# Key-value sums over four tiles of tokens, and other figures for DMA additions in the planner of a gated attention kernel

## The chip, the cores and the metric

One core of one Trainium2 chip. The metric is the device time of one execution in microseconds. Before the change it is 724.36 us, the median of three executions (723.66 to 725.03).

## What is computed

Two attention branches over the same x (2048 tokens of 512, 32 heads of 16), mixed by a gate for each token. Projections and final weights are left out here except where they show:

```python
g = sigmoid((x * gate_w).sum(-1, keepdims=True))
# branch A, softmax attention
q, k, v = split_heads(x @ A_wqkv)
a = merge(softmax(q @ k.T * 16 ** -0.5) @ v) @ A_wo
# branch B, linear attention; w_phi is 16 x 16 for each head
q, k, v = split_heads(x @ B_wqkv)
phi = lambda t: concat(softmax(t @ w_phi), softmax(-(t @ w_phi)))   # 32 features
kv, z = phi(k).T @ v, phi(k).sum(tokens)
b = merge((phi(q) @ kv) / (phi(q) @ z + 1e-6)) @ B_wo
out = g * a + (1 - g) * b
```

## The kernel before

**Branch A** is nearly all of the work: 2048 x 2048 scores for each of 32 heads. A *unit* is 128 keys by 512 queries of one head; four units (four heads that sit in four row groups of TensorE) make a step, and 512 steps make the kernel. `_qk` (L1185 in `_scores`) writes scores of two units at a time to a ring of four PSUM banks, and `_exp` (L1233) takes their exponential on ScalarE into `ET`, a ring of 16 units in SBUF. `_pv` (L1296 in `_values`) multiplies a step's `ET` by V and adds it to a PSUM bank that is held for 16 steps; this group of 16 steps is one head slot of 512 queries. The exponential of a unit must wait until the value product of the unit 16 places before it has read its slot.

ScalarE is not alone with the exponentials. `NUMS` gives for each of the 32 groups a number of *batches* of four units that VectorE makes instead. VectorE writes the exponential's bits by arithmetic: one multiply-add from PSUM to 16-bit whole numbers in a tile `va` (L1043), and constants added to the whole numbers for further approximations in tiles `vb` (L1072 on VectorE, L1085 on GpSimd). Some of these additions are done by DMA: GpSimd issues a transfer that adds the constant tile `steps` to `va` or `vb` (L1077, 512 KB). Each batch takes four value products of its own (`pvx`, also L1296), and those of an added tile wait for the transfer to land.

**Branch B** goes through key tiles of 128 tokens first: `_b_pair` projects two tiles and makes their features in one of two slots of `bq` (L1457, L1475 to L1498 and, on ScalarE, the exponential L1494); `_b_v` makes the values (`VB`, four slots); `_b_kv` (L1573) multiplies features by values for two halves of the heads, and VectorE adds each result to `kvacc` (L1581, L1584). Then `_b_kvbd` lays the sums out, and the query tiles follow in pairs (L1613, L1633, L1663, L1668).

Projections of q and k for branch A are L808 (L816 and L855 for the first block of tokens), of v L923. L1303 and L1205 are filler matmuls on zeros or into banks that are overwritten, which keep TensorE busy. At the end `_out` projects both branches (L808 again) and stores the rows.

**The order of the work** is made by `Plan` when the program is built: every operation carries a cost, a latency, a due time and dependencies, and `order()` picks, over and over, the operation that can start first by its own clock, the more urgent one among equals. The order that it finds is then each engine's fixed program; semaphores make the engines wait for each other. Three of its tables and figures matter here:

- `SEEDS`: 64 numbers; every eight steps the next one shifts the due times of all operations that are still open by up to a few steps, at random. It is a choice among many orders of nearly equal merit.
- `SLIP`: `_late` holds back any TensorE work that would end after the moment at which the ring's next scores must start, and `SLIP` shifts that moment.
- `FIRST`, `MOVES`, `LANDED`: the planner's figures for one addition by DMA. Its transfer starts `FIRST` after the issue or when the one before it has moved, takes `MOVES`, and has landed `LANDED` later. Value products on the added tile are put in the order behind that moment.

```python
self.chan = max(t + self.FIRST, self.chan) + o.moves
o.lat = self.chan + self.LANDED - o.end
```

Of the kernel before, what the change touches and what calls it, by code (L numbers as in the profile page):

```python
# [70 lines left out]
class Plan:  # L71
# [6 lines left out]
    SWITCH, PASS, STEP = 0.097, 0.2155, 0.004  # L78
    SPAN, SHARE, FILL = 3.0, 0.58, 0.2155
    PAD, PADS, OVER = 0.45, 2, 0.2  # L80
    SLIP, GAPS, FLOOR = -0.015, 0.65, 0.46

    def __init__(self):
        self.ops = []
# [58 lines left out]
        self.ops.append(o)  # L143
        return o

    SEEDS = (46439, 36297, 2531, 40950, 971, 19659, 43523, 55019, 18035, 35534, 32147, 43513, 5583, 38153, 15135, 20962, 59679, 30439, 26213, 19105, 29455, 34877, 55135, 21414, 3210, 43195, 29993, 1363, 20599, 10691, 26101, 32053, 19915, 10799, 30427, 37694, 56714, 13257, 35679, 20623, 23887, 52907, 36031, 9619, 51019, 11311, 52185, 0, 13385, 43491, 31707, 19759, 44590, 53230, 9789, 22249, 59009, 3577, 57594, 35439, 52351, 16746, 45215, 2875)
    EVERY = 8
    FIRST, LANDED, TURN, HOLD = 1.5, 1.5, 1.9, 30.0

    def shift(self):  # L150

        if len(self.SEEDS) <= self.drawn or self.now < self.EVERY * self.drawn:
            return
        s = self.SEEDS[self.drawn]
        self.drawn += 1
# [329 lines left out]
class _Kernel:  # L485
# [11 lines left out]
    P_Q, P_MUL, P_NEG = 1, 1, 1  # L497
    P_REC, P_SUM = 0, 4
    P_BACK, RATIO, BV = 0, 1, 8
    DEN, KV2, P_MAX = 1, 0, 0  # L500
    P_SUB = 0
    REND = 4
    RINGOUT = 1
# [8 lines left out]
    LAST, FIRST_OUT, NEXT_OUT, DEP_OUT = 0, 3, 0, 2  # L512
    ALONE, EARLY = 12, 10
    C_MIX, C_POOL, SPREAD = 15.5, (0.2, 0.0011), 0.9
    C_ADD, MOVES, ADD_AT, PVD, U3 = 0.9, 2.9, -1, 0, 2
    L_MIX, L_BACK, L_PHIT, L_ONTB = 6.5, 0.4, 0.9, 0.4
    TWOS, BEGIN, SPLIT, PSPLIT = 2, 44, 262, 1
    PHIT2, ONTB2, C_PHIT2, C_ONTB2 = 1, 1, 2.3, 1.9
# [460 lines left out]
                prio=100))  # L979
        self.b_gB.writers = done  # L980

    NUMS = (1, 4, 5, 4, 4, 5, 4, 5, 4, 5, 4, 6, 5, 4, 4, 5, 5, 5, 5, 4, 4, 5, 4, 5, 4, 5, 5, 5, 6, 6, 5, 4)

    def _plan_vector(self):

        NT, away = self.NT, []
        for g in range(self.NPACK // NT):
            n = self.NUMS[g]
            rest = self.REND if g == self.NPACK // NT - 1 else self.REST
# [885 lines left out]
```

## Time and profile before

| | |
|---|---|
| median of three executions | 724.36 us (723.66 to 725.03) |
| the profiled execution | 723.53 us |
| its span, first to last instruction | 721.7 us |
| exponentials of branch A (L1233) | 734, of which 4 of half width |
| batches made by VectorE | 146 of four units |
| DMA additions (L1077) | 157 |
| additions to `kvacc` (L1584) | 14, and two first copies (L1581) |

PE is TensorE's matmuls, PEld its weight loads, DVE VectorE, ACT ScalarE, POOL GpSimd, SP the engine that issues other DMAs. A row of a group gives line, engine, operation, tiles written and read, shapes and count; then busy us and the mean ns of one; then the engine's idle us just ahead of them, with what ended most of it. A row of a timeline gives start, length, engine, line, and in brackets the idle time before it and its releaser. Records of ACT and DVE overlap their neighbours, so the distance of starts is shorter than a record.

### The profile page before, as it was taken

The numbers are of one execution on the slowest core, as the hardware profiler recorded it, in microseconds if no ns is written. First come the engines' busy times: TensorE is split into PE (matmuls) and PEld (weight loads), VectorE is DVE, ScalarE is ACT, GpSimd is POOL, SyncE is SP. The second block draws the span as 40 slices with busy tenths as digits, with TensorE's granted clock in tenths as the row PEclk, the third lists the DMA queues.
The fourth block names the chain that finished last, engine by engine and source line by source line (L and its number), as shares of the span: only waits on it lengthen the run. The fifth ranks groups of instructions, "written<-read, shape, count | busy, mean of one in ns | idle before, by whom it ended". The sixth has DMA issues, their size and how long they took to land.

```text
span 721.7 us, 17384 instructions
## 1 busy us (share of the span) xinstructions
PE 694.0 (96%) x7312; PEld 211.7 (29%) x7375; DVE 691.5 (96%) x1143; ACT 706.4 (98%) x756; POOL 447.8 (62%) x567
## 2 busy tenths in 40 slices
PE   8999999999999999999999999999999999999998
PEld 3332232222333222222222233232323232223222
DVE  4999999999999999999999999999999999999997
ACT  5999999999999999999999999999999999999996
POOL 3332566665675747485768775768758678477552
PEclk9999999999999999999999999999999999999999
DMA  9623676684966778966768877678678577868873
GB/s 226 155 50 74 123 136 119 116 158 94 189 117 118 147 143 169 187 121 118 140 122 157 166 146 146 105 147 159 114 135 163 112 155 147 151 129 150 165 139 88
DMA packets 68557, 99.17 MB, mean 137 GB/s; under 512 B 42752, under 2 KB 47872, under 8 KB 68480
## 3 DMA queue, kind: packets, MB, share of 16 engines
q0 software_dynamic: 22608, 82.32, 60.4%
q1 hardware_dynamic: 44000, 14.96, 10.3%
q8 instruction: 57, 0.93, 0.5%
q10 hardware_dynamic: 1872, 0.79, 0.5%
q14 instruction: 20, 0.16, 0.1%
HBM read 4.21 MB, written 2.10 MB: 9 GB/s over the span
## 4 chain that ended last, share of the span: by engine, by line
ACT 65%; PE 20%; DVE 7%; DMA 3%; POOL 2%; issue 1%; SPq 1%; POOLq 0%
ACT ET L1233 63%; PE ps L1185 7%; PE ps L1296 7%; PE ps L808 5%; ACT bq L1494 2%; DVE va L1043 2%; DVE vb L1072 1%; DMA va<-steps 1%; DMA vb<-steps 1%; SPq L673 1%; DMA xT<-in_A_x_dram 1%; DVE va_vb L1043 1%; POOL va L1077 0%; DVE onB L1668 0%; PE ps L923 0%
## 5 line engine op out<-in xcount | busy, mean ns | idle before, releaser
L1233 ACT ACTIVATE ET<-ps 128x1024 bf16<-128x1024 f32 (+1 forms) x734 | 677.1, 1084 | 3.1 <-PE ps L1185 1.6
L1043 DVE TENSOR_SCALAR va<-ps 128x512 uint16<-128x512 f32 (+1 forms) x438 | 312.6, 745 | 13.1 <-PE ps L1185 12.1
L1185 PE MATMUL ps<-qT,kT 32*128 32x512 bf16 (+1 forms) x2052 | 292.3, 384 | 13.3 <-ACT ET L1233 7.7
L1077 POOL DMA_DIRECT2D va<-steps x106 | 107.1, 1061 | 103.6 <-DVE vb L1072 50.2
L1185 PEld LDWEIGHTS ps<-qT,kT 32*128 32x128 bf16 x2052 | 74.0, 91 | 277.5 <-ACT ET L1233 255.8
L1296 PE MATMUL ps<-ET,V 128*32 128x512 bf16 x1464 | 141.9, 388 | 0.7 <-DVE va L1043 0.7
L1072 DVE TENSOR_SCALAR vb<-va 128x2048 uint16<-128x2048 uint16 x147 | 100.3, 695 | 0.2 <-PE ps L1296 0.2
L1296 PE MATMUL ps<-va,V 128*32 128x512 bf16 x984 | 92.3, 384 | 0.3 <-DVE vb L1072 0.3
L1296 PE MATMUL ps<-vb,V 128*32 128x512 bf16 x896 | 84.1, 384 | 0.6 <-DMA vb<-steps 0.3
L1085 POOL TENSOR_TENSOR vb<-vb,steps 128x512 int32<-128x512 int32 x50 | 64.0, 1299 | 26.7 <-DVE vb L1072 19.2
L1296 PEld LDWEIGHTS ps<-ET,V 128*32 128x32 bf16 x1464 | 36.4, 94 | 66.9 <-issue 59.0
L808 PE MATMUL ps<-WB,xT 128*128 128x512 bf16 x164 | 49.6, 383 | 3.6 <-issue 2.4
L1498 POOL TENSOR_TENSOR btree<-btree 128x512 f16<-128x512 f16 (+1 forms) x32 | 30.3, 947 | 22.2 <-DVE vb L1072 12.7
L1303 PE MATMUL ps<-kT,zero 128*32 128x512 bf16 x492 | 43.1, 383 | 0.0
L1077 POOL DMA_DIRECT2D vb<-steps x28 | 33.7, 1203 | 8.2 <-PE ps L808 3.7
L808 PE MATMUL ps<-xT,WA 128*128 128x512 bf16 x102 | 32.4, 384 | 2.0 <-issue 1.3
L1043 DVE TENSOR_SCALAR va_vb<-ps 128x512 uint16<-128x512 f32 (+1 forms) x47 | 33.7, 734 | 0.1
L1296 PEld LDWEIGHTS ps<-va,V 128*32 128x32 bf16 x984 | 24.3, 95 | 27.9 <-issue 20.8
L1494 ACT ACTIVATE bq<-bq 128x2048 bf16<-128x2048 bf16 x16 | 31.4, 1960 | 0.0
L899 POOL TENSOR_SCALAR qT<-qT,mask 128x512 bf16<-128x512 bf16 x30 | 22.8, 761 | 12.1 <-DVE qT L895 6.2
L1296 PEld LDWEIGHTS ps<-vb,V 128*32 128x32 bf16 x896 | 22.0, 95 | 24.3 <-issue 14.3
L1043 DVE TENSOR_SCALAR va_wt<-ps 128x512 uint16<-128x512 f32 (+1 forms) x36 | 25.9, 738 | 0.1
(123 smaller groups left out, 721.2 us busy)
## 6 DMA issues: line engine op xcount, KB each, us to landing
va<-steps POOLq DMA_DIRECT2D x106, 512.0 KB, 6.3
vb<-steps POOLq DMA_DIRECT2D x28, 512.0 KB, 7.0
va_wt<-steps POOLq DMA_DIRECT2D x10, 512.0 KB, 5.9
va_vb<-steps POOLq DMA_DIRECT2D x10, 512.0 KB, 5.5
WB<-in_B_wqkv_dram SPq DMA_DIRECT2D x1, 1536.0 KB, 8.2
vb_on<-steps POOLq DMA_DIRECT2D x3, 512.0 KB, 6.7
out_dram<-outt SPq DMA_DIRECT2D x12, 128.0 KB, 6.3
WA<-in_A_wqkv_dram SPq DMA_DIRECT2D x2, 384.0 KB, 4.4
```

The costliest lines, as they stand in the source:

```text
L808: return e.matmul(out, lhs, rhs, start=start, stop=stop)
L899: x = self.plan.op("POOL", lambda e, side=side: e.tensor_scalar(self.qT[:, s0 + side, :], raw, self.mask[:, side:side + 1], 0.0, op0=ALU.m ...
L1043: bits = lambda e, to, src: e.tensor_scalar(to, src, SCALE * LOG2E * 128.0, float(ORIGIN), op0=ALU.mult, op1=ALU.add)
L1072: o = op("DVE", lambda e: e.tensor_scalar(whole(dst), whole(va), float(by), None, op0=ALU.add), 0.16 + n * QCH * 0.00026, reads=reads, wri ...
L1077: o = self.dma("POOL", f"add{number}_{k}", lambda e: e.dma_start(tile[:, 0:n], self.steps[:, 0:n], accum_op=ALU.add), cost=self.C_ADD, rea ...
L1085: o = op("POOL", lambda e, lo=lo, hi=hi: e.tensor_tensor(whole(v3)[:, lo:hi].bitcast(I32), whole(v1)[:, lo:hi].bitcast(I32), whole(self.st ...
L1185: return e.matmul(out[:, cols], self.kT[32 * i:32 * i + 32, cp, kt * TOK:(kt + 1) * TOK], self.qT[32 * i:32 * i + 32, s, cols], start=True ...
L1233: o = plan.op("ACT", lambda e: e.activation(self.ET[:, a % NS:a % NS + n, cols], self.ps[:, a % NR:a % NR + n, cols], ACT.Exp, scale=SCALE ...
L1296: ins = e.matmul(self._bank(ot)[32 * i:32 * i + 32, :], v[:, v0:v0 + 32], tile, start=(kt == 0), stop=(kt == self.NT - 1), tile_position=( ...
L1303: ins = e.matmul(self._bank(ot)[32 * i:32 * i + 32, :], self.zero[:], self.kT[:, 0, 0:QCH], start=False, stop=False, tile_position=(0, 32 ...
L1494: op("ACT", lambda e: e.activation(flat, flat, ACT.Exp), 1.789, reads=[b], writes=[b], name="b_exp", prio=due + 1)
L1498: + [("b_sum", two(128 * n), lambda e, n=n: e.tensor_tensor(half[:, :, 0:n], half[:, :, 0:n], half[:, :, n:2 * n], ALU.add), (n <= self.P_ ...
```

## The change

`KV2` makes `_b_kv` wait for four tiles of tokens and add their products in PSUM, so 4 results for each half go to `kvacc` where 8 did. The planner takes additions to start, move and land sooner, and `SLIP` is stricter. `NUMS` gives VectorE 145 batches for 146, with one batch more in the first group and one fewer in the last. `SEEDS` is a new list throughout.

```diff
-    SLIP, GAPS, FLOOR = -0.015, 0.65, 0.46
+    SLIP, GAPS, FLOOR = -0.04, 0.65, 0.46
...
-    FIRST, LANDED, TURN, HOLD = 1.5, 1.5, 1.9, 30.0
+    FIRST, LANDED, TURN, HOLD = 1.4, 1.2, 1.9, 30.0
...
-    DEN, KV2, P_MAX = 1, 0, 0
+    DEN, KV2, P_MAX = 1, 1, 0
...
-    C_ADD, MOVES, ADD_AT, PVD, U3 = 0.9, 2.9, -1, 0, 2
+    C_ADD, MOVES, ADD_AT, PVD, U3 = 0.9, 2.85, -1, 0, 2
...
-    NUMS = (1, 4, 5, 4, 4, 5, 4, 5, 4, 5, 4, 6, 5, 4, 4, 5, 5, 5, 5, 4, 4, 5, 4, 5, 4, 5, 5, 5, 6, 6, 5, 4)
+    NUMS = (2, 4, 4, 5, 5, 5, 4, 4, 5, 5, 5, 4, 5, 6, 4, 6, 4, 6, 4, 4, 4, 4, 4, 5, 4, 4, 5, 4, 5, 6, 6, 3)
```

With the new due times nearly every row of the order moves. Three places on TensorE follow. Row by row they have line, operation, tile written and read, shape, and a count where equal ones follow each other.

The first is the start, up to the first value product (L1296). L1185 are scores of the ring and of the first batches, L808 the projections of k, L923 those of v. Before, the last 12 rows up to it:

```order
L808 MATMUL ps<-xT,WA 128x512 x2
L1185 MATMUL ps<-qT,kT 128x512 x2
L923 MATMUL ps<-WA,xT 128x2x128 x4
L1185 MATMUL ps<-qT,kT 128x512 x4
L923 MATMUL ps<-WA,xT 128x2x128 x4
L808 MATMUL ps<-xT,WA 128x512
L1185 MATMUL ps<-qT,kT 128x512 x2
L923 MATMUL ps<-WA,xT 128x2x128 x4
L1185 MATMUL ps<-qT,kT 128x512 x3
L923 MATMUL ps<-WA,xT 128x2x128 x4
L1185 MATMUL ps<-qT,kT 128x512 x3
L1296 MATMUL ps<-ET,V 32x512 x8
```

Now, likewise the last 12 rows (one more L923 x4 stands two rows ahead of them, and a filler L1205 ahead of the first full-width scores):

```order
L923 MATMUL ps<-WA,xT 128x2x128 x4
L1185 MATMUL ps<-qT,kT 128x512 x3
L923 MATMUL ps<-WA,xT 128x2x128 x4
L1185 MATMUL ps<-qT,kT 128x512 x3
L923 MATMUL ps<-WA,xT 128x2x128 x4
L808 MATMUL ps<-xT,WA 128x512
L1185 MATMUL ps<-qT,kT 128x512 x3
L808 MATMUL ps<-xT,WA 128x512 x2
L1185 MATMUL ps<-qT,kT 128x512 x3
L808 MATMUL ps<-xT,WA 128x512
L923 MATMUL ps<-WA,xT 128x2x128 x8
L1296 MATMUL ps<-ET,V 32x512 x4
```

Ahead of the first value product stand 24 matmuls of L923 where 16 stood; the other eight were right behind it. The matmuls of L808 between the first full-width scores and it are eight in both; four of them now stand behind the first L923, where one did.

The second is the end, from the last scores on. `ET` is ScalarE's tile, `va`, `vb`, `WB` those of VectorE's batches; L808 are the output projections of both branches. Before:

```order
L1185 MATMUL ps<-qT,kT 128x512 x2
L808 MATMUL ps<-WoA,onTA 128x512 x3
L808 MATMUL ps<-WoB,WT 128x512 x2
L1296 MATMUL ps<-ET,V 32x512 x4
L1296 MATMUL ps<-va_100,V_67 32x512 x4
L1296 MATMUL ps<-va_97,V_67 32x512 x4
L1296 MATMUL ps<-vb_104,V_67 32x512 x4
L808 MATMUL ps<-WoB,WT 128x512 x2
L808 MATMUL ps<-WoA,onTA 128x512 x6
L808 MATMUL ps<-WoB,WT 128x512 x4
L808 MATMUL ps<-WoA,onTA 128x512 x7
```

Now:

```order
L1185 MATMUL ps<-qT,kT 128x512 x2
L1296 MATMUL ps<-ET,V 32x512 x4
L1296 MATMUL ps<-va_100,V_67 32x512 x4
L1296 MATMUL ps<-ET,V 32x512 x4
L1296 MATMUL ps<-WB,V_67 32x512 x4
L1296 MATMUL ps<-ET,V 32x512 x8
L1296 MATMUL ps<-va_vb,V_67 32x512 x4
L808 MATMUL ps<-WoA,onTA 128x512 x4
L808 MATMUL ps<-WoB,WT 128x512 x8
L808 MATMUL ps<-WoA,onTA 128x512 x7
```

Seven value products follow the last scores where four did, and 19 projections where 24 did; behind the last exponential's own product (the last four of `ET`) one product stands ahead of the projections, not three.

The third is the first key-value sum (L1573, features `bq` by values `VB`), both halves of the heads. Before:

```order
L1185 MATMUL ps<-qT,kT 128x512 x2
L1573 MATMUL ps<-VB,bq 128x68 x8
L1185 MATMUL ps<-qT,kT 128x512 x4
L1296 MATMUL ps<-ET,V 32x512 x4
L1296 MATMUL ps<-vb_101,V_67 32x512 x4
L1296 MATMUL ps<-ET,V 32x512 x4
L1185 MATMUL ps<-qT,kT 128x512 x2
L1573 MATMUL ps<-VB,bq 128x68 x8
L1185 MATMUL ps<-qT,kT 128x512 x2
```

Now:

```order
L1185 MATMUL ps<-qT,kT 128x512 x2
L1573 MATMUL ps<-VB,bq 128x68 x16
L1185 MATMUL ps<-qT,kT 128x512 x3
L1296 MATMUL ps<-ET,V 32x512 x4
L1296 MATMUL ps<-vb_103,V_67 32x512 x4
L1296 MATMUL ps<-va_97,V 32x512 x4
L1185 MATMUL ps<-qT,kT 128x512 x3
L1296 MATMUL ps<-ET,V 32x512 x4
L1296 MATMUL ps<-vb_102,V_67 32x512 x4
L1185 MATMUL ps<-qT,kT 128x512 x2
L1573 MATMUL ps<-VB,bq 128x68 x16
L1185 MATMUL ps<-qT,kT 128x512 x3
```

A half's sum is one piece of 16 matmuls over four tiles where it was two pieces of 8 over two; there are 8 pieces of 16 in all, where 12 of 8 and 2 of 16 (two halves next to each other) stood.

More of the change, by code (lines that the diff above doesn't have):

```diff
@@ L144, in op @@
         return o
-    SEEDS = (46439, 36297, 2531, 40950, 971, 19659, 43523, 55019, 18035, 35534, 32147, 43513, 5583, 38153, 15135, 20962, 59679, 30439, 26213, 19105, 29455, 34877, 55135, 21414, 3210, 43195, 29993, 1363, 20599, 10691, 26101, 32053, 19915, 10799, 30427, 37694, 56714, 13257, 35679, 20623, 23887, 52907, 36031, 9619, 51019, 11311, 52185, 0, 13385, 43491, 31707, 19759, 44590, 53230, 9789, 22249, 59009, 3577, 57594, 35439, 52351, 16746, 45215, 2875)
+    SEEDS = (45959, 51639, 22027, 0, 55887, 32675, 45763, 19658, 23974, 59913, 48419, 50277, 38610, 29071, 54255, 16561, 28074, 8627, 30494, 39995, 2986, 24098, 45178, 38933, 24915, 36789, 25403, 3823, 12338, 46755, 9994, 14699, 28830, 13382, 17277, 24473, 47187, 46797, 29842, 24695, 38758, 30863, 50967, 40255, 29411, 50751, 30934, 36618, 21679, 35286, 15639, 9075, 55554, 30865, 8986, 8939, 45463, 37302, 49375, 44231, 4706, 52075, 15731, 25615)
     EVERY = 8
-    FIRST, LANDED, TURN, HOLD = 1.5, 1.5, 1.9, 30.0
+    FIRST, LANDED, TURN, HOLD = 1.4, 1.2, 1.9, 30.0
     def shift(self):
```

## The prediction, made blind

> **What bounds the kernel now.** First the page: busy time by engine, the chain that ended last, and the two dearest groups.
>
> ```profile
> span 721.7 us, 17384 instructions
> PE 694.0 (96%) x7312; PEld 211.7 (29%) x7375; DVE 691.5 (96%) x1143; ACT 706.4 (98%) x756; POOL 447.8 (62%) x567
> ACT 65%; PE 20%; DVE 7%; DMA 3%; POOL 2%; issue 1%; SPq 1%; POOLq 0%
> L1233 ACT ACTIVATE ET<-ps 128x1024 bf16<-128x1024 f32 (+1 forms) x734 | 677.1, 1084 | 3.1 <-PE ps L1185 1.6
> ```
>
> Three engines are nearly full, so the shares do not choose between them. The idle time before the exponentials does: 3.1 us before 734 of them, and the chain runs through ACT for 65%. Next the windows, three of them (columns: length; then busy us and instructions of PE, PEld, DVE, ACT, POOL; clock, DMA share, GB/s).
>
> ```profile
> 60.00:100.00 40.00, 39.12 (x361) 11.47 (x364) 38.78 (x68) 39.95 (x44) 20.44 (x29) 1.00 0.63 119
> 340.00:380.00 40.00, 38.12 (x425) 11.01 (x425) 38.26 (x64) 40.00 (x44) 27.38 (x40) 1.00 0.69 131
> 660.00:700.00 40.00, 39.18 (x443) 11.41 (x444) 38.36 (x64) 40.00 (x45) 21.22 (x21) 1.00 0.85 161
> ```
>
> ACT is busy for the whole of each, while PE and DVE each leave 0.8 to 1.9 us. But records of ACT overlap, so "busy" hides small delays. For the true pace I take runs without a break from the chain in order of time (start, length, what).
>
> ```profile
> 183.61 1.79 ACT bq L1494
> 185.40 40.35 ACT ET L1233 x44
> ```
>
> 40.35 / 44 = **0.917 us** for one exponential of two units, and 1.79 for one of branch B's 16. Now ACT's beginning and end, from its timeline.
>
> ```profile
> 9.35 3.02 ACT L1233 ACTIVATE ET<-ps 128x512 bf16<-128x512 f32 x4 [0.53 <-PE ps L1185]
> 12.76 3.83 ACT L1233 ACTIVATE ET<-ps 128x1024 bf16<-128x1024 f32 x4 [0.39 <-PE ps L1185]
> 17.64 17.59 ACT L1233 ACTIVATE ET<-ps 128x1024 bf16<-128x1024 f32 x19 [1.05 <-PE ps L1296]
> ...
> 699.31 14.09 ACT L1233 ACTIVATE ET<-ps 128x1024 bf16<-128x1024 f32 x15
> 717.66 0.60 ACT L1819 ACTIVATE xT<-ps 128x512 bf16<-128x512 f32 x1 [4.26 <-PE ps L808]
> ```
>
> From 17.64 to 713.40 lie 695.8 us. Of the 734 exponentials, 4 halves and 6 whole ones are before 17.64; 724 x 0.917 = 663.9, 16 x 1.79 = 28.6, the gate's small one 0.3: 692.8, and the last record is 0.1 longer than the pace. So ACT loses only **2.8 us** in 696. The time is a head of 17.64, ACT's work, those 2.8, and an end of 721.7 - 713.4 = 8.3. I price the change in these four pieces. The sum starts from this execution's own 723.53 us (span and 1.8 around it); the median of the three runs is 724.36, 0.83 more, and I put the difference onto the median.
>
> **ACT's work: +1.83 us.** One batch of four units less for VectorE (145 for 146) gives ACT four units, two exponentials more (its order has 732 whole ones for 730): 2 x 0.917 = 1.83. No cover exists, since ACT is never idle. The Trainium skill's page "ScalarE: Activation LUTs", section "What ACT_TABLE_LOAD costs", gives 186 ns + 0.833 ns an element less an overlap of 93; for 1024 elements that would be 946 ns and two would cost 1.89. The row's 0.917 decides.
>
> **The head: +0.65 us.** The ring of ET holds 16 units, so the seventh whole exponential waits for the first value product (L1296): that is the 1.05 in the row at 17.64. What PE does ahead of it (PE's timeline):
>
> ```profile
> 9.63 0.38 PE L808 MATMUL ps<-xT,WA 128*128 128x512 bf16 x1
> 10.00 0.39 PE L1185 MATMUL ps<-qT,kT 32*128 32x512 bf16 x2
> ...
> 12.01 0.39 PE L808 MATMUL ps<-xT,WA 128*128 128x512 bf16 x1 [0.44 <-DMA xT<-in_A_x_dram]
> 12.33 0.39 PE L1185 MATMUL ps<-qT,kT 32*128 32x512 bf16 x2
> 12.88 0.38 PE L808 MATMUL ps<-xT,WA 128*128 128x512 bf16 x1 [0.16 <-issue]
> ...
> 17.19 0.61 PE L1296 MATMUL ps<-ET,V 128*32 128x512 bf16 x8
> 17.74 1.05 PE L923 MATMUL ps<-WA,xT 128*128 128x256 bf16 x8
> 18.62 0.38 PE L808 MATMUL ps<-xT,WA 128*128 128x512 bf16 x1
> ```
>
> Between 9.63 and the first L1296 stand 8 pieces of scores and 8 matmuls of L808 in both orders. New are eight matmuls of L923 that stood behind it (17.74 to 18.62: 0.88) and a filler, L1205 (one full-width matmul, 9.63 to 10.00: 0.37). Gone are the wait for the third block of x, 0.44, because the fifth L808 comes later, and one of 0.16. 0.88 + 0.37 - 0.44 - 0.16 = +0.65, so ACT resumes at about 18.3. Nothing later gives that back while ACT is full. Bounds: 0, if the planner's order meets PE idle that I do not see, and 1.25, if neither wait goes.
>
> **The end: -0.44 us.** PE after the last exponential (713.40), and the chain's last pieces:
>
> ```profile
> 713.45 0.40 PE L1296 MATMUL ps<-ET,V 128*32 128x512 bf16 x4
> 713.67 0.60 PE L1296 MATMUL ps<-va,V 128*32 128x512 bf16 x8
> 714.11 0.39 PE L1296 MATMUL ps<-vb,V 128*32 128x512 bf16 x4
> 714.43 0.60 PE L808 MATMUL ps<-WoB,WT 128*128 128x512 bf16 x2
> ```
> ```profile
> 714.50 4.22 PE ps L808 x19
> 718.74 0.60 ACT xT L1819
> ```
>
> Four value products, two steps of 0.22 (713.45 to 713.67, 713.67 to 714.11 for two) and a last one of 0.32 with the change of shape to the projections, fill 0.98 us ahead of the 19 projections that the chain runs through. In the new order five pieces (value products, where five projections were) lie between the last scores and the last exponential's own product; they fit into that exponential as the five did, 0.22 each. Behind it comes only one more product, then again 19 projections. Two products fewer: 2 x 0.22 = 0.44 less. DVE's chain from the last product to the last projections starts as much earlier. Bounds: 0, if another wait ends last there, and 0.66.
>
> **The key-value sums: 0.** DVE loses 8 additions (8 x 0.35, from the starts below) and one batch's work, PE and PSUM get pieces twice as long. The trace has two pieces of 16 already, where both halves stood together:
>
> ```profile
> 137.92 0.39 PE L1185 MATMUL ps<-qT,kT 32*128 32x512 bf16 x2
> 138.24 0.67 PE L1573 MATMUL ps<-VB,bq 128*128 128x68 bf16 x16
> 138.84 0.39 PE L1185 MATMUL ps<-qT,kT 32*128 32x512 bf16 x2
> ```
> ```profile
> 139.11 0.77 DVE L1584 TENSOR_TENSOR kvacc<-kvacc,ps 128x272 f32<-128x272 f32 x2
> 139.80 1.03 DVE L1480 TENSOR_TENSOR btree<-btree 128x512 bf16<-128x512 bf16 x1
> ```
>
> Scores to scores is 0.92 there, just ACT's pace, and at all eight places the new order puts a piece of 16 alone between two pieces of scores. It hides behind one exponential, with no room left: 0 is the value, and if each of the 8 ran over by the piece of pv that it pushes out (0.22), +1.8. A gain needs ACT to be waiting for DVE; at most it is the 2.8 us.
>
> **The figures of the additions: 0, and at most +14.** 157 additions are issued; their landings and PE's waits for them (the view of line L1077):
>
> ```profile
>   PEld ps L1296: 2.9, 9
>   PE ps L1296: 0.3, 1
> DMA to landing us min/median/max: 4.5/6.4/13.1
> ```
>
> A lone one is planned to land 1.5 + 2.9 + 1.5 = 5.9 us after its issue, now 1.4 + 2.85 + 1.2 = 5.45. Put beside the 157 issues and landings of this trace, the old formula was early 13 times, by 3.6 us in sum; the new one would be 39 times, by 17.4. PE's waits of 3.2 us cost ACT 0.11 in one place (the exponential ending at 146.03). At the same share the 13.8 us more cost ACT 0.4; if all came through, 14. I take the low end, with the stricter SLIP (0.025 us earlier for each piece of PE beside the scores) set against it: 0.
>
> **Sum.** 1.83 + 0.65 - 0.44 + 0 + 0 = +2.04: this execution would take 725.6, and the median 724.36 + 2.04 = **726.4 us**.
>
> **Rivals.**
> 1. *Landings late.* PE works in order, so a value product waiting for an addition holds up the scores behind it; ACT has one exponential's length in hand. If a third of the 13.8 us reaches ACT: +4.6, 731.0. For it: 39 early figures. Against: only 0.11 of 3.2 came through before.
> 2. *ACT's small delays go.* DVE is lighter by 2.8 us of additions and a batch, and SLIP is stricter. With half of the 2.8 us gone: 726.4 - 1.4 = 725.0, no change.
> 3. *Faster.* The same mechanism in full: a lighter DVE returns PSUM banks sooner everywhere, in the head too, so that the head's wait of 1.05 goes with the 2.8 us: 724.36 + 1.83 - 0.44 - 2.8 - 1.05 = 721.9. It turns the sign from 722.9 on, that is if no more than 1.0 of those 3.85 us is left. The Trainium skill's "Perfetto Trace Analysis", section "Optimizing Scalar/DVE Operations", says that grouping into larger operations improves throughput if the engine is saturated; DVE's 96% would suggest it. By that the 8 additions come off the time. The windows speak against: DVE has 1.2 to 1.7 us in 40 to spare where ACT has none.
> 4. *Bursts.* The sums over four tiles hold both slots of bq until the fourth tile, so branch B's pairs come two by two, and a double burst of DVE work delays scores of the batches: eight pieces at 0.22, as priced above, +1.8: 728.2.
>
> **How the numbers follow.** Forecast (725.4 to 727.4) 0.45; landings late 0.15; bursts 0.13; small delays go 0.23; faster 0.04. A measurement of this kernel tells about 0.2%, 1.45 us, from no change. Faster than 722.9: 0.04. Within, up to 725.8: rival 2 and a fifth of the forecast, 0.33. Slower: 0.63. The range runs from 724.0 (rival 2 with two thirds of the delays gone) to 730.5, a little short of the first rival's 731.0, which leaves about 2 in 10 out.
>
> **What would show it.** ACT's exponentials: 736 at the same 0.917. The row with the wait for L1296 near 18.3, its idle time at 1.7 where it was 1.05 (less if the 0.39 at 12.76 went). From the last exponential to the span's end 7.9 for 8.3. ACT's work between head and end against its rows: 2.8 lost again. The forecast is wrong if PE's waits for additions go far above 3.2 us with gaps in ACT behind them, or if gaps stand at the eight L1573 pieces; and on the other side, if the lost time falls under 1 us.

## The result, and the profile after

The changed kernel takes **729.5 us** (median of five executions, 728.56 to 732.95) where the kernel before takes 724.01 (five, 723.30 to 725.03): slower by a ratio of 1.0081 with an interval of 1.0057 to 1.0106 (the medians alone give 1.0076). The direction and the range of the prediction held. The size did not: +5.5 us by the medians, where +2.0 was forecast, so most of the loss is a term that I had put at nothing.

First the page: span, busy time, the chain that ended last, and the exponentials.

```profile
span 727.7 us, 17303 instructions
PE 692.4 (95%) x7269; PEld 210.6 (29%) x7336; DVE 690.1 (95%) x1131; ACT 708.3 (97%) x758; POOL 442.4 (61%) x565
PE 37%; DVE 27%; ACT 21%; DMA 10%; POOL 4%; issue 1%; POOLq 0%
L1233 ACT ACTIVATE ET<-ps 128x1024 bf16<-128x1024 f32 (+1 forms) x736 | 678.9, 1084 | 6.9 <-PE ps L1185 4.2
```

PE and DVE did less than before (692.4 for 694.0, 690.1 for 691.5), and the span is 6 us longer. The chain shows where to look: it ran through ACT for 65% of its length, now for 21%, and DMA has 10% of it where it had 3%. ACT's idle time ahead of the exponentials rose from 3.1 to 6.9 us, 4.2 of it ended by scores (L1185). Now ACT's timeline at both ends.

```profile
8.23 1.09 ACT L1233 ACTIVATE ET<-ps 128x512 bf16<-128x512 f32 x2 [0.47 <-PE ps L1185]
9.85 1.08 ACT L1233 ACTIVATE ET<-ps 128x512 bf16<-128x512 f32 x2 [0.53 <-PE ps L1185]
11.26 5.61 ACT L1233 ACTIVATE ET<-ps 128x1024 bf16<-128x1024 f32 x6 [0.32 <-PE ps L1185]
19.13 2.86 ACT L1233 ACTIVATE ET<-ps 128x1024 bf16<-128x1024 f32 x3 [2.27 <-PE ps L1296]
...
711.17 8.63 ACT L1233 ACTIVATE ET<-ps 128x1024 bf16<-128x1024 f32 x9
723.63 0.60 ACT L1819 ACTIVATE xT<-ps 128x512 bf16<-128x512 f32 x1 [3.83 <-PE ps L808]
```

The last exponential ends at 711.17 + 8.63 = 719.80. The same account as for before gives 4 halves and 6 whole ones ahead of 19.13, so 726 x 0.917 + 28.6 + 0.3 = 694.6 of work and 0.1 for the last record, in 719.80 - 19.13 = 700.7 us: **5.9 us lost, where before lost 2.8**. So the profiled execution (729.52) stands to before's (723.53) like this:

| piece | predicted | measured |
|---|---|---|
| head (17.64, now 19.13) | +0.65 | +1.49, 0.5 of it ahead of the first exponential |
| ACT's work, two exponentials | +1.83 | +1.83 |
| lost between head and last exponential | 0 | +3.1 |
| end (8.3, now 727.7 - 719.8 = 7.9) | -0.44 | -0.4 |
| sum | +2.04 | +6.0 |

The view of the additions' line (L1077) names what waits, and PE's waits name how long the longest are (us in total, times, longest). First after:

```profile
  PEld ps L1296: 9.0, 16
  PE ps L1296: 3.5, 8
DMA to landing us min/median/max: 4.5/6.2/12.0
```
```profile
PEld ps L1296 <- DMA va<-steps: 5.6, 11, 1.0
```

And the same row of before's waits, with its longest one, which is in another row:

```profile
PEld ps L1296 <- DMA va<-steps: 1.7, 6, 0.4
PEld ps L1296 <- DMA vb<-steps: 1.0, 2, 0.8
```

The landings themselves are no later (median 6.2 for 6.4). The value products come sooner: 12.5 us of waits in both rows where there were 3.2. The two rows must not be read as a sum of time, though, since a product's weight load (PEld) and its matmuls (PE) wait for the same landing. Weight loads waited 9.0 us for 2.9, and the matmuls themselves 3.5 us for 0.3. Of the 16 waits of weight loads eight are over 0.6 us, where one of nine was; the longest is 1.0 us, where it was 0.8. What one of them does (ACT, PE and its weight loads, in order of time):

```profile
229.04 1.94 ACT L1233 ACTIVATE ET<-ps 128x1024 bf16<-128x1024 f32 x2
229.96 0.39 PE L1296 MATMUL ps<-ET,V 128*32 128x512 bf16 x4
230.85 0.10 PEld L1296 LDWEIGHTS ps<-va,V 128*32 128x32 bf16 x4 [1.00 <-DMA va<-steps]
230.86 0.40 PE L1296 MATMUL ps<-va,V 128*32 128x512 bf16 x4 [0.51 <-DMA va<-steps]
231.19 0.40 PE L1185 MATMUL ps<-qT,kT 32*128 32x512 bf16 x4
231.62 2.85 ACT L1233 ACTIVATE ET<-ps 128x1024 bf16<-128x1024 f32 x3 [0.65 <-PE ps L1185]
```

PE works in order. The product of `va` stands ahead of four scores, its addition lands late, the scores start at 231.19, and ACT, which was through at 230.98, waits 0.65.

### The profile page after: what moved, and what is told of

Read it like the earlier page. It is cut to its first block, busy times and chain, and to the rows that moved or that the text cites. A ratio compares the mean times of both kernels' runs of the same rounds, so it can differ in the third digit from the quotient of the medians.

```text
span 727.7 us, 17303 instructions
## 1 busy us (share of the span) xinstructions
PE 692.4 (95%) x7269; PEld 210.6 (29%) x7336; DVE 690.1 (95%) x1131; ACT 708.3 (97%) x758; POOL 442.4 (61%) x565
## 4 chain that ended last, share of the span: by engine, by line
PE 37%; DVE 27%; ACT 21%; DMA 10%; POOL 4%; issue 1%; POOLq 0%
ACT ET L1233 20%; PE ps L1185 13%; PE ps L1296 12%; DVE va L1043 11%; PE ps L808 8%; DMA va<-steps 6%; DVE vb L1072 4%; DMA vb<-steps 3%; DVE va_wt L1043 1%; DMA va_vb<-steps 1%; PE ps L1303 1%; DVE bq L1483 1%; POOL va L1077 1%; POOL btree L1498 1%; PE ps L923 1%
## 5 line engine op out<-in xcount | busy, mean ns | idle before, releaser
L1043 DVE TENSOR_SCALAR va<-ps 128x512 uint16<-128x512 f32 (+1 forms) x436 | 311.6, 745 | 13.8 <-PE ps L1185 12.4
L1185 PE MATMUL ps<-qT,kT 32*128 32x512 bf16 (+1 forms) x2052 | 291.8, 384 | 17.3 <-ACT ET L1233 12.8
L1077 POOL DMA_DIRECT2D va<-steps x106 | 110.9, 1084 | 78.3 <-DVE vb L1072 36.1
L1185 PEld LDWEIGHTS ps<-qT,kT 32*128 32x128 bf16 x2052 | 73.6, 91 | 282.6 <-ACT ET L1233 259.7
L1296 PE MATMUL ps<-ET,V 128*32 128x512 bf16 x1468 | 142.4, 388 | 1.4 <-DVE va L1043 1.0
L1072 DVE TENSOR_SCALAR vb<-va 128x2048 uint16<-128x2048 uint16 x145 | 99.1, 700 | 0.1
L1296 PE MATMUL ps<-va,V 128*32 128x512 bf16 x976 | 92.0, 383 | 2.3 <-DMA va<-steps 1.9
L1296 PE MATMUL ps<-vb,V 128*32 128x512 bf16 x892 | 84.3, 384 | 1.4 <-DMA vb<-steps 1.0
L1085 POOL TENSOR_TENSOR vb<-vb,steps 128x512 int32<-128x512 int32 x50 | 67.3, 1362 | 28.3 <-PE ps L1296 12.2
L1296 PEld LDWEIGHTS ps<-ET,V 128*32 128x32 bf16 x1468 | 36.7, 94 | 66.7 <-issue 57.6
L808 PE MATMUL ps<-WB,xT 128*128 128x512 bf16 x162 | 50.2, 384 | 3.6 <-issue 2.9
L1498 POOL TENSOR_TENSOR btree<-btree 128x512 f16<-128x512 f16 (+1 forms) x32 | 33.2, 1038 | 14.9 <-DVE btree L1496 8.6
L1303 PE MATMUL ps<-kT,zero 128*32 128x512 bf16 x464 | 39.8, 384 | 0.0
L1077 POOL DMA_DIRECT2D vb<-steps x28 | 28.3, 1010 | 11.4 <-PE ps L1296 7.7
L1043 DVE TENSOR_SCALAR va_vb<-ps 128x512 uint16<-128x512 f32 (+1 forms) x44 | 31.9, 731 | 2.6 <-PE ps L1185 2.4
L899 POOL TENSOR_SCALAR qT<-qT,mask 128x512 bf16<-128x512 bf16 x30 | 21.2, 708 | 21.1 <-DVE bq L1483 6.4
L1296 PEld LDWEIGHTS ps<-va,V 128*32 128x32 bf16 x976 | 24.6, 96 | 27.2 <-issue 15.7
L808 PE MATMUL ps<-xT,WA 128*128 128x512 bf16 x98 | 30.4, 383 | 1.7 <-issue 1.6
L1296 PEld LDWEIGHTS ps<-vb,V 128*32 128x32 bf16 x892 | 22.1, 95 | 26.9 <-issue 16.5
L1043 DVE TENSOR_SCALAR va_wt<-ps 128x512 uint16<-128x512 f32 (+1 forms) x39 | 28.7, 748 | 0.0
```

The source lines that it names most:

```text
L808: return e.matmul(out, lhs, rhs, start=start, stop=stop)
L899: x = self.plan.op("POOL", lambda e, side=side: e.tensor_scalar(self.qT[:, s0 + side, :], raw, self.mask[:, side:side + 1], 0.0, op0=ALU.m ...
L1043: bits = lambda e, to, src: e.tensor_scalar(to, src, SCALE * LOG2E * 128.0, float(ORIGIN), op0=ALU.mult, op1=ALU.add)
L1072: o = op("DVE", lambda e: e.tensor_scalar(whole(dst), whole(va), float(by), None, op0=ALU.add), 0.16 + n * QCH * 0.00026, reads=reads, wri ...
L1077: o = self.dma("POOL", f"add{number}_{k}", lambda e: e.dma_start(tile[:, 0:n], self.steps[:, 0:n], accum_op=ALU.add), cost=self.C_ADD, rea ...
L1085: o = op("POOL", lambda e, lo=lo, hi=hi: e.tensor_tensor(whole(v3)[:, lo:hi].bitcast(I32), whole(v1)[:, lo:hi].bitcast(I32), whole(self.st ...
```

## The experiments

**Theory:** value products that now stand close behind, or ahead of, their additions' landings hold up the scores, and ACT loses some 3 to 4 us there. **Rivals:** the order alone (the head, a pair of exponentials in the wrong order) makes the loss; or branch B's eight pieces of key-value sums do.

**1. Additions that land early, in both orders.** The order is kept to the last instruction; each addition moves one of the tile's four parts and the other three are left out of the sum, so that it lands sooner.

```diff
-e.dma_start(tile[:, 0:n], self.steps[:, 0:n], accum_op=ALU.add)
+e.dma_start(tile[:, 0:1], self.steps[:, 0:1], accum_op=ALU.add)
```

On the changed kernel:

> The changed kernel with the same order on every engine, where each of the 157 additions moves a quarter of its tile (one of four rows of it; the other three rows of that batch miss the constant, so that part of the computation is left out). Theory (additions land later than the order counts on): TensorE's waits for additions, 12.5 us in the profile of after (9.0 and 3.5), fall under 1 us, ACT's lost time between head and end falls from about 6.2 to about 3.5 us, and the median goes from 729.5 to about 726.8. Rival (the new order is crowded in itself, the additions are only what happens to be waited for): waits fall likewise but another wait takes their place, and the time stays within 0.8 us of 729.5.

On the kernel before, as a control:

> The kernel before with the same order and each addition a quarter of its size (the rest of those tiles left out), as a control. Theory (before, additions cost ACT next to nothing): no change, 723.7 to 724.2, since 3.2 us of TensorE's waits cost ACT 0.11. Rival (smaller transfers help in another way, by less load on the memory or on GpSimd's issuing): faster by 1 us or more here too.

Measured: the changed order 725.58 us, ratio to before 1.0018 (1.0009 to 1.0027); before's order 724.12, ratio 1.0001 (0.9992 to 1.0009). In the changed order no product waits for an addition any more:

```profile
DMA to landing us min/median/max: 2.6/2.9/4.9
```
```profile
18.65 2.85 ACT L1233 ACTIVATE ET<-ps 128x1024 bf16<-128x1024 f32 x3 [2.27 <-PE ps L1296]
...
719.46 0.60 ACT L1819 ACTIVATE xT<-ps 128x512 bf16<-128x512 f32 x1 [3.83 <-PE ps L808]
```

The head's 2.27 is still there. The last exponential ends at 719.46 - 3.83 = 715.63, so from 18.65 on ACT loses 697.0 - 694.7 = 2.3 us where the changed kernel lost 5.9. **Late additions cost the changed order 3.9 us by the medians** (3.6 by ACT's account), more than the 2.7 expected, and before's order nothing clear of noise, so lighter transfers gain nothing by themselves. What is left, +1.55, is close to the sum that I had: two exponentials, a longer head, a shorter end.

ACT's delays, place by place, say the same. Each exponential's end was set against the end before it and the pace. In the changed kernel 2.8 us of delay stand within 2 us behind the 16 waits for additions, at eight of them; before it is 0.1, at one of nine. Another 0.8 us (0.62 at 429.9 us, 0.20 at 194.2) stands where the run with quarter additions has no delay. The theory's mechanism is shown; that the figures and not the new list put the products there is not yet.

**2. The two exponentials alone.** Before's kernel issues the 251st and the 451st exponential twice, the copy into an unused place.

```diff
-        o = plan.op("ACT", lambda e: e.activation(
-            self.ET[:, a % NS:a % NS + n, cols], self.ps[:, a % NR:a % NR + n, cols], ACT.Exp, scale=SCALE),
+        def run(e):
+            if k in (250, 450):
...
+                e.activation(spare[:, 0:2 * QCH].rearrange("p (a b) -> p a b", a=2), self.ps[:, a % NR:a % NR + n, cols], ACT.Exp, scale=SCALE)
+            return e.activation(
+                self.ET[:, a % NS:a % NS + n, cols], self.ps[:, a % NR:a % NR + n, cols], ACT.Exp, scale=SCALE)
+        o = plan.op("ACT", run,
```

> The kernel before with two of its exponentials issued twice (the 251st and the 451st; the extra result goes to a place that nothing reads). Theory (ACT is full, two exponentials more cost their pace): +1.83 us, 725.8. Rival (ACT has some cover, its 2.8 us of delays take part of it up): +1.0 or less.

726.0 us, ratio 1.0028 (1.0016 to 1.0039, that is 1.2 to 2.8 us): +1.97 for 1.83 worked out. In the profiled execution the head alone was 1.6 us later (19.23 for 17.64), and from it to the last exponential ACT took 697.2 us where before took 695.8. So ACT has little cover, some 0.4 us at most in that trace. The Trainium skill's page "ScalarE: Activation LUTs", section "What ACT_TABLE_LOAD costs", gives 186 ns + 0.833 ns an element, less 93 ns of overlap back to back, from which 1.89 us is an estimate for the two. This run cannot tell the two prices apart; the trace's pace of 0.917 us for one decides.

**3. The head mended.** In the changed order the filler is dropped and a projection put in its place, the first value product goes ahead of the eight L923, and two exponentials that stand in the wrong order (near 390 us) are put right.

```diff
-            p.order()
+            p.order(); self._mend()
...
+        pe[first].filled = 0
+        pe.insert(first, pe.pop(proj))
...
+        pe.insert(to, pe.pop(pv))
...
+            if x.startswith("exp") and y.startswith("exp") and int(x[3:]) > int(y[3:]):
+                act[i], act[i + 1] = act[i + 1], act[i]
```

> The changed kernel with three places of its order mended by hand after the planner, no work left out: the filler ahead of the first full-width scores is dropped and a projection of k put there instead; the first value product moves ahead of the eight projections of v in front of it; the one pair of exponentials that stands in swapped order (near 389 us) is put right. Theory (the head's order costs 1.0 us, the swapped pair 0.59): ACT resumes about 1.0 us earlier against its first exponential, no delay near 389, and the median goes from 729.5 to about 727.9. Rival (the head gives nothing, since VectorE's bank for the first value product comes no earlier): only 0.6 us, 728.9.

729.22 us, ratio 1.0073 (1.0059 to 1.0086): 0.3 us less than the changed kernel, which is within the spread of either. ACT's head:

```profile
9.49 6.69 ACT L1233 ACTIVATE ET<-ps 128x512 bf16<-128x512 f32 x8 [0.54 <-PE ps L1185]
17.70 1.94 ACT L1233 ACTIVATE ET<-ps 128x1024 bf16<-128x1024 f32 x2 [1.53 <-PE ps L1296]
20.19 4.81 ACT L1233 ACTIVATE ET<-ps 128x1024 bf16<-128x1024 f32 x5 [0.55 <-PE ps L1185]
```

The wait for the value product did go from 19.13 to 17.70, but ACT waits again at 20.19, since the L923 that the product passed now stand ahead of the next scores, twelve in a row on PE:

```profile
17.59 1.48 PE L923 MATMUL ps<-WA,xT 128*128 128x256 bf16 x12
```

Further on, the delay of 0.59 us near 390 is gone, and ACT's delays behind some additions are longer (0.73 us at 400, where the changed kernel has 0.34 at 401); in sum they are 2.8 us, as without the mend. This mend undoes one wait and makes another, so it is a weak test of the head; but the rival is refuted as the main cause, since the loss stays here and most of it goes in experiment 1, where the order is untouched.

**4. One part undone, the order drawn anew.** Four kernels: before with the new figures of the additions alone (`b_figs`), the changed kernel with the old ones (`a_figs`), before with `KV2` alone (`b_kv`), the changed kernel without it (`a_kv`). The edits are lines of the change's diff. `b_figs`, and reversed `a_figs`:

```diff
-    FIRST, LANDED, TURN, HOLD = 1.5, 1.5, 1.9, 30.0
+    FIRST, LANDED, TURN, HOLD = 1.4, 1.2, 1.9, 30.0
-    C_ADD, MOVES, ADD_AT, PVD, U3 = 0.9, 2.9, -1, 0, 2
+    C_ADD, MOVES, ADD_AT, PVD, U3 = 0.9, 2.85, -1, 0, 2
```

`b_kv`, and reversed `a_kv`:

```diff
-    DEN, KV2, P_MAX = 1, 0, 0
+    DEN, KV2, P_MAX = 1, 1, 0
```

> The kernel before with only the planner's three figures of the additions changed to the new ones (an addition counted as landed 1.4 us + 1.2 us for the first, 2.85 us of moving for the next, in place of 1.5, 1.5 and 2.9); seeds, SLIP, pair count and the four-tile option stay. The seeds then shift due times of another order, so the time itself is a draw; the measure is TensorE's waits for additions, in the rows of the value products (before: 2.9 us in 9 waits and 0.3 us in 1; changed kernel: 9.0 us in 16 and 3.5 us in 8). Theory, the new figures put value products ahead of their additions: 8 us or more in 16 waits or more, and ScalarE's groups with a delay after the head rise by 2 us or more. Rival, the waits come from this one drawn order: 2 to 6 us, as before.

> The changed kernel with only the planner's three figures of the additions put back. Measure as in the run beside it. Theory: TensorE's waits for additions fall from 12.5 us to about 3 to 5 us. Rival: they stay above 8 us, whatever the figures. Time: 727 us by the theory if the drawn order costs nothing else (729.5 less some 2.6 us), 729.5 by the rival; other draws move either by several us.

> The kernel before with only the key-value sums over four tiles of tokens at a time, the rest kept, so that the order is drawn anew by the same seeds. Theory, the sums themselves are free: no delay of ScalarE's exponentials of over 0.1 us beside the eight-piece groups, and TensorE's waits for additions stay at 2 to 6 us; time 724 to 726 by that alone. Rival, eight products in a row hold up the scores: a delay of 0.2 us or more at each of the eight-piece groups, some 1.8 us in all.

> The changed kernel with only the key-value sums put back to two tiles at a time; the new figures stay. Theory: TensorE's waits for additions stay at 8 us or more in 16 waits or more, since they come from the figures, and the time stays at 728 to 731. Rival, the sums are what costs: waits fall to some 3 us and the time to 726 or 727.

| kernel | median us | ratio to before | PE's waits for additions, both rows |
|---|---|---|---|
| `b_figs` | 791.84 | 1.093 (1.0886 to 1.0974) | 14.3 us in 32 |
| `a_figs` | 818.4 | 1.1306 (1.1285 to 1.1326) | 12.9 us in 8 |
| `b_kv` | 819.01 | 1.1331 (1.1268 to 1.1394) | 15.9 us in 22 |
| `a_kv` | 783.16 | 1.0807 (1.0741 to 1.0873) | 15.7 us in 26 |

(The last column adds two rows that count the same landing twice, as said above.) All four miss by far more than the effect in question, so none of them tells its part's price. They show something else: **with a part of the numbers changed, the list of due-time shifts fits no more**, in four cases of four, and ACT stands still for whole stretches. The longest in `b_kv`, ACT's row and then PE's:

```profile
419.45 2.86 ACT L1233 ACTIVATE ET<-ps 128x1024 bf16<-128x1024 f32 x3 [19.86 <-PE ps L1296]
```
```profile
402.86 0.62 PE L1296 MATMUL ps<-va,V 128*32 128x512 bf16 x4 [1.98 <-DMA va<-steps]
407.33 3.59 PE L808 MATMUL ps<-WB,xT 128*128 128x512 bf16 x8 [3.85 <-POOL VB L1432]
411.71 1.99 PE L1573 MATMUL ps<-VB,bq 128*128 128x68 bf16 x32 [0.79 <-DVE VB L1434]
413.52 4.69 PE L808 MATMUL ps<-WB,xT 128*128 128x512 bf16 x16
```

Branch B's work has come due in one piece; no scores stand between 402.86 and 418, and PE waits in it three times. The waits for additions do not sort by the figures either. With the new ones `b_figs` and `a_kv` have the 8 us or more that were expected, but with the old ones `b_kv` has 15.9 us and `a_figs` 12.9, where 2 to 6 and 3 to 5 were expected. So an ill-fitting list makes such waits by itself, and in this way the figures cannot be told from the list. For `KV2` the changed kernel's own trace answers. All eight pieces of 16 have rows like this one, ACT's row first:

```profile
147.07 8.42 ACT L1233 ACTIVATE ET<-ps 128x1024 bf16<-128x1024 f32 x9
```
```profile
149.13 0.39 PE L1185 MATMUL ps<-qT,kT 32*128 32x512 bf16 x2
149.45 0.67 PE L1573 MATMUL ps<-VB,bq 128*128 128x68 bf16 x16
150.05 0.39 PE L1185 MATMUL ps<-qT,kT 32*128 32x512 bf16 x3
```

Scores to scores is 0.92 again, ACT runs on without a break, and no exponential within 2.6 us of any of the eight ends late. That rival falls.

**5. Products moved, the order otherwise kept.** With the order held, nothing is drawn. In before's order 62 of the products of added tiles go ahead by one group of scores, as far as the new figures allow; in the changed order 49 go back by one.

```diff
-            p.order()
+            p.order(); self._sooner()
...
+            chan = max(o.start + 1.4, chan) + 2.85 * o.moves / self.MOVES
+            due[id(o)] = chan + 1.2
...
+            if row and pe[j - 1].kind == "col" and pe[j - 1].end >= own and pe[j-1].end < own + 0.6:
+                pe.insert(j, pe.pop(i))
```

> The kernel before with its own order kept, and 62 of its 157 value products of added tiles moved ahead by one group of scores (0.65 to 1 us by the planner's clock), never ahead of where the new figures count the addition as landed. Nothing else is moved; no list is drawn anew. Theory, products put near their landings wait, and ScalarE gets it: TensorE's waits for additions rise from 3.2 us to 8 us or more, time 725.5 to 727. Rival, the waits stay on TensorE, whose scores have room (a quarter of the bytes changed nothing in this order): waits rise, time 723.6 to 724.6.

729.33 us, ratio 1.0066 (1.0052 to 1.008): +4.7, about as slow as the changed kernel. PE's waits for additions in it:

```profile
  PEld ps L1296: 8.1, 17
  PE ps L1296: 1.8, 6
```
```profile
PEld ps L1296 <- DMA va<-steps: 5.8, 12, 0.8
```

9.9 us for 3.2 in both rows; the longest is 0.8, as long as before's longest, but six are over 0.6 where one was. The theory's time was exceeded, so a second cause may be in it: a product put ahead also holds up the scores that it passes. The same order with quarter additions (one part of four, the rest left out) takes the landings away:

> The order of before with the same 62 value products moved ahead (729.3 us with whole additions, 4.7 us over before), and each addition moves the first quarter of its tile alone; the rest of the sum is left out. Theory, the price of the early place is the wait for the landing: the time falls back to 724 to 725, as the control on before's own order stood (724.12 us). Rival, the early product crowds the scores behind it, whatever lands: 727 to 729.5.

726.15 us, ratio 1.0028 (1.0019 to 1.0038). So of the 0.66%, about 0.38% (2.8 us) is the landing and 0.28% (2.0 us) what is left without it, the crowding by the rival's account: neither expectation alone, with the landing the larger. The other direction:

> The changed kernel with its own order kept, and 49 of the 101 value products that stand ahead of the landing by the old figures moved back by one group of scores (mostly 0.65 to 1.5 us); the other 52 stay, since scores of the next batch that write the same tile stand right behind them, or the next place is over 1.6 us away. Theory: TensorE's waits for additions fall from 12.5 us to 6 to 9, and the time by 1 to 2 us, to 727.5 to 728.5. Rival, a product moved back waits for less but crowds the next group: waits fall, time 729 to 730 or more.

> The changed kernel's order with the same 49 products moved back (734.3 us with whole additions, 4.8 us over the changed kernel), each addition moving a quarter of its tile, the rest left out. Theory, moving back costs by crowding and by freeing tiles later, and the landings that remained in the way are some 2 us: 730 to 733 us, above the 725.6 us of the changed order with quarter additions. Rival, what rose there was waits for other landings: 725 to 727.

734.34 us, ratio 1.0135 (1.0121 to 1.0148), and with quarter additions 732.54, ratio 1.0116 (1.01 to 1.0131). Waits for additions did fall, to 5.8 us, and the time rose by 4.8, further than the rival had it. Without any landing in the way this order is still 7.0 us over the changed one with quarter additions (725.58), as its theory expected. What ACT and PE wait for instead, in the kernel with whole additions, and one place of it:

```profile
ACT ET L1233 <- PE ps L1185: 5.2, 14, 0.6
```
```profile
396.86 1.21 DVE L1072 TENSOR_SCALAR va<-va 128x2048 uint16<-128x2048 uint16 x1
398.12 0.40 PE L1296 MATMUL ps<-va,V 128*32 128x512 bf16 x4 [0.41 <-DVE va L1072]
398.45 0.40 PE L1185 MATMUL ps<-qT,kT 32*128 32x512 bf16 x4
398.88 1.94 ACT L1233 ACTIVATE ET<-ps 128x1024 bf16<-128x1024 f32 x2 [0.39 <-PE ps L1185]
```

Here a product waits for a step of VectorE (L1072) that took 1.21 us, where the median of its line is 0.68, with no idle time ahead of it; the scores behind the product come late, and ACT waits 0.39. That VectorE runs late because a product that reads a tile later frees it later is one explanation. This place does not show it. GpSimd's waits for products ahead of its additions did rise from 33.2 to 42.4 us, but with quarter additions only from 32.2 to 35.6, where the order loses more. So what makes up the 7.0 us is not shown. My expectation of 1 to 2 us gained is refuted: moving these 49 products by hand does not mend the order.

## Why the prediction was right in direction and wrong in size

- **What bounds the kernel: right.** ACT has little cover; two more exponentials cost 1.97 us by experiment 2.
- **ACT's work and the end: right**, +1.83 and -0.4 in the trace.
- **Key-value sums: right at 0.** Six L1584 of 0.43 stand where fourteen stood, and nothing ran over at the eight places. Whether the lighter VectorE gave something back is left with rival 2.
- **The head: mis-sized**, +0.65 predicted and +0.99 from the first exponential on. What I missed is a wait. The order shows a filler but not what it waits for:

```profile
10.51 0.39 PE L1205 MATMUL ps<-kT 128*128 128x512 bf16 x1 [0.47 <-ACT ET L1233]
10.83 0.39 PE L1185 MATMUL ps<-qT,kT 32*128 32x512 bf16 x2
```

  It needs the ring place that ACT is still reading; the projection that stood there before did not, and filled that time. The other 0.5 us lies ahead of the first exponential (8.23 for 7.73). It differs between executions (7.76 in experiment 1's, with the same order), so I do not put it down to the change.
- **The figures of the additions: this step failed.** The prediction let 0.11 of every 3.2 us of waits reach ACT, as before, and so put the term at 0. (Its own numbers give 0.47 us for the 13.8 us more that it expected; it wrote 0.4.) It cost 3.6 to 3.9 us. The 3.2 was no length of time, since it counts one landing in two rows, and the share is no constant. By weight loads the waits rose by 6.0 us, and 2.7 us more of delay stand right behind them; by the matmuls they rose by 3.2. Nor does the length of a wait decide alone. Before's longest cost ACT nothing:

```profile
499.16 1.91 ACT L1494 ACTIVATE bq<-bq 128x2048 bf16<-128x2048 bf16 x1
500.96 2.85 ACT L1233 ACTIVATE ET<-ps 128x1024 bf16<-128x1024 f32 x3
501.45 0.10 PEld L1296 LDWEIGHTS ps<-vb,V 128*32 128x32 bf16 x4 [0.81 <-DMA vb<-steps]
502.03 0.10 PEld L1185 LDWEIGHTS ps<-qT,kT 32*128 32x128 bf16 x4 [0.46 <-ACT ET L1233]
```

  ACT had just had one of branch B's exponentials (1.79 us), which let PE get ahead, and the scores behind the product still had to wait for ACT. The changed kernel's 0.90 at 425.43 cost nothing either, with another of those beginning at 425.55. Its other seven waits over 0.6 us, and one of 0.40, came where there was no such room, and cost 0.13 to 0.75 us each. Rival 1 was this mechanism, at 731.0 with a chance of 0.15.
- **Luck.** The band of the forecast, 725.4 to 727.4, missed; the range holds the result because its top, 730.5, was set near rival 1. Its low end does not follow from what it names: 726.4 less two thirds of 2.8 is 724.5, not 724.0. Setting `SLIP` against the landings had no row behind it, and nothing like that shows.
- **Rival 2** (ACT's small delays go) is true for some 0.5 us net: 2.3 us lost in experiment 1's changed order, 2.8 in before's. Of the 2.3, 1.0 stands at two places that the new order made (0.59 at the swapped exponentials, 0.44 at 533), so the other small delays fell by about half. The runs do not tell whether VectorE's lighter work, `SLIP` or the new list did that.

What stays open is how much of the 3.9 us the figures own. The planner never puts a product ahead of the landing that it assumes: in before's order the median of 157 products is 0.41 us behind it by the planner's own clock, in the changed order 0.39. By the old figures 101 of those in the changed order would stand ahead of the landing, by up to 0.70. Against the landings of the changed kernel's trace the new figures are too early for 20% of the additions and the old ones for 8%. And of the 16 products that waited in it, 14 are among the 101, with all eight that ACT paid for: the old figures would have kept them out of those places. That, and experiment 5's +4.7 us for moving products ahead in a fixed order, speak for the figures; experiment 4 shows that a list can make such waits with the old figures too. A run with the new figures and a list fitted to them again, next to one with the old figures and such a list, would tell, and was not made. No kernel here beats the one before.

## What to carry to other kernels

A wait on an engine that works in order does not reach the bounding engine in proportion. Here it cost nothing where the scores behind it had time in hand, and up to 0.75 us of its 1.00 where they had none. So ask of each wait what room there is at its place; neither the sum of the waits nor the longest tells. A planner's figure for a transfer is a promise to everything behind the waiting instruction. The figures that 20% of the landings miss went with the loss here, and those that 8% miss did not, which speaks for setting them by the late landings; a proof would need the two runs named above. And where an order was fitted to a set of numbers, changing one number and planning again did not test that number here: hold the order and change what the instructions do.

## What the runs showed of the hardware that was not expected

An addition of a quarter of a tile lands 2.9 us after its issue (median) where a whole one takes 6.2 to 6.4, and at least 2.6 where a whole one takes at least 4.5. A straight line through the two shortest leaves about 2.0 us that do not depend on the bytes, an estimate from two sizes. And TensorE's granted clock, 1.00 in before's windows, was lower in `b_kv` in the stretch where PE stood waiting (columns as in the prediction's windows):

```profile
400.00:421.00 21.00, 14.25 (x108) 5.73 (x106) 10.00 (x18) 1.55 (x2) 11.70 (x20) 0.63 0.12 23
```

Shorter windows give 0.50 from 400 to 415 and 1.00 from 416 on. There the work itself took twice as long: the eight L808 at 407.33 take 3.59 us, 0.45 each, where the 19 of before's end (4.22 us, in the prediction) take 0.22. The fall lies between 398 and 399 (0.82 in that window), so ahead of the three waits shown in experiment 4; PE had stood 2.32 us until 397.59. That standing still brings the clock down fits this order of events, and no run here tests it.
